# Row maxima of two key halves taken by one VectorE instruction over two PSUM banks, in the first batch of an attention and FFN kernel

## The chip, the cores and the metric

One core of a Trainium2 chip runs the whole program. The metric is the device time of one execution in microseconds (us). The engines go by their short names: PE (TensorE, matrix products), PEld (its weight loads, recorded apart), DVE (VectorE), ACT (ScalarE), POOL (GpSimd) and SP (SyncE, which issues nearly all DMAs). Matrix products land in PSUM, which this program uses as eight banks of 128 partitions by 512 fp32 numbers; the other engines read their results from there.

## The reference

Block-sparse attention over 4 batches of 8 heads (768 positions, head size 64) feeds an FFN of width 2048 with a piecewise quadratic activation.

```
scores = 0.125 * q @ k.T                 # per batch and head, 768 x 768
scores = where(mask, scores, -1e9)       # mask by blocks of 32: band, edges, 3 sampled blocks a row
scores = scores - max(scores, axis=-1)
attn = exp(scores); attn = attn / (sum(attn, axis=-1) + 1e-9)
x = (attn @ v) -> [3072, 512]
h = x @ w_in                             # 512 -> 2048
g = where(h >= 1, h, where(h <= -1, 0, (h + 1)**2 / 4))
out = g @ w_out                          # 2048 -> 512
```

## The kernel before

Precise products are made from pairs: a number is split into a rounded high part and a low remainder, and the matmuls add up high times high and the cross terms. The two weight matrices come as 64-bit numbers and are converted and split on the chip by `convert`: ACT takes an absolute value (L168), DVE does four steps on the bits (L169, L170, L172, L174) on 128x512 tiles, ACT casts to the high part (L196), DVE subtracts (L180).

**A head.** Its K and Q, with 24 rows that carry the mask, stand in tiles KA and QA, of which there are two sets, so that two heads can be in work. The load L214 brings the data, ACT casts the high part, DMAs move it into KA and QA (L221 and following), DVE forms the low part (`lo`, L228, a 128x768 subtraction). Then, for each of six query tiles of 128 rows and two halves of 384 keys, `max_mm` (L267) makes approximate scores in a PSUM bank, and `max_red` (L272) takes their maxima over the keys into one column of mc: twelve matmuls, twelve reductions. `max_col` (L276) merges the two halves into mr, `max_turn` (L280) transposes mr on PE, and `max_row` (L283) writes the negative maxima as six more rows of QA; with these rows the score matmuls subtract the maximum by themselves. In head 0 these last three steps come in two rounds of three query tiles.

Then the scores follow: for each half of 384 queries and six key tiles a pair of matmuls (L303, L304), the exponential on ACT (L308), and the value matmul (L333), which the profile records as two instructions. The six value products of a half add up in one bank, po or, for the second half in a wide head, oa2. ACT copies the result out (L351, L353); after each second head the sums are turned to reciprocals (L372, through two DMAs), and DVE and ACT make the FFN's input x from it (L387, L395).

**Heads 0 to 7, the first batch, are called wide.** No FFN runs beside them yet, since its input isn't there; the conversion of w_in runs beside them. Heads 8 to 31 run beside the FFN of the batch before, and there the maxima's banks are pa, as the scores' are.

**The FFN** (`moe`) runs in eight halves of 384 tokens: 16 tiles of the hidden width each, `l1` (L457 to L459) into hp, the activation on ACT and DVE (L463 to L478), `l2` (L485 to L487) into three output tiles oa0, oa1, oa2, one for each 128 tokens, which are kept over the 16 tiles. `o_copy` (L496, L498) copies them out by ACT; in the last half of all the second goes by DVE.

**PSUM.** Three banks pa, one po, one hp, and one each of oa0, oa1, oa2: eight. While no FFN runs, the wide heads use its banks: `bank(wide, use)` deals them out in turn, by the table RINGS (L567): scores go to oa0, oa1, hp, maxima to the three pa.

**Order.** Every step enters a list with a due time (`at`), the list is sorted by it, and a scheduler that sees dependencies and buffers sets the final order of each engine from it. An engine works its own order off without overtaking: whatever stands behind a waiting instruction waits too.

## Time and profile before

| | us |
|---|---|
| median of 3 runs | 984.24 (982.64 to 984.28) |
| the profiled execution | 983.67 |
| its span, first to last instruction | 981.8 |

Mean granted PE clock in the profiled execution: 0.998 of full speed. An instruction's row shows its start and length, its engine, its line, its output and inputs, and in brackets the idle time ahead of it on its engine with what ended that. The chain of waits goes back from the last instruction, at each step to what released it. The maxima's reductions in all heads hold 202.5 us of DVE time, of 747.5 busy. The first batch's heads lie roughly between 10 and 150 us, the first FFN half's end is at 287.6 (first output copy), and the last output copy starts at 977.65.

### The profile page before, as it was taken

Reading aid. Unit: us, or ns where it says so; the run is one execution under the profiler, and the core shown is the slowest. Engines: PE = TensorE matmul, PEld = TensorE weight load, DVE = VectorE, ACT = ScalarE, POOL = GpSimd, SP = SyncE. Lnnn points to the kernel's source line nnn. Section 1 sums busy time; section 2 is a strip of 40 time slices with the busy share of each in tenths; the row PEclk is TensorE's granted clock in tenths of the full one; section 3 lists DMA queues with packets and bytes.
Section 4 is the critical chain, followed back from the end, with each engine's and each line's share of the span. In section 5 each row is a group of like instructions: output and inputs, shape, how many; then the busy total and the mean of one; then the engine's idle time right before and its main releaser. Section 6 shows DMA issues by size and latency. Waiting matters only on the chain.

```text
span 981.8 us, 14556 instructions
## 1 busy us (share of the span) xinstructions
PE 942.5 (96%) x4687; PEld 828.1 (84%) x4687; DVE 747.5 (76%) x1403; ACT 636.5 (65%) x1302; POOL 251.8 (26%) x229
## 2 busy tenths in 40 slices
PE   5899899999889999999999999999999999999998
PEld 3666677877779899999989998998999999899997
DVE  5888999889998888978788888888888885422222
ACT  3667777677667676767677767776767676433433
POOL 1000000023334343433434343343434343000000
PEclk9999999999999999999999999999999999999999
DMA  6756677754355444645555443645445432433432
GB/s 195 205 149 189 196 209 225 259 180 139 123 182 163 145 143 133 182 139 153 159 150 182 131 150 116 199 137 175 138 142 178 125 115 89 154 130 129 160 129 97
DMA packets 56216, 154.43 MB, mean 157 GB/s; under 512 B 9612, under 2 KB 17952, under 8 KB 56140
## 3 DMA queue, kind: packets, MB, share of 16 engines
q1 hardware_dynamic: 56100, 153.48, 51.5%
q8 instruction: 37, 0.61, 0.3%
q14 instruction: 39, 0.32, 0.1%
q10 hardware_dynamic: 40, 0.03, 0.0%
HBM read 100.92 MB, written 14.81 MB: 118 GB/s over the span
## 4 chain that ended last, share of the span: by engine, by line
PE 85%; DVE 7%; ACT 3%; DMA 2%; issue 2%; SPq 0%; ACTq 0%; DVEq 0%
PE oa L485 8%; PE oa L487 8%; PE oa L486 8%; PE hp L457 8%; PE hp L459 7%; PE hp L458 7%; PE pa L267 7%; PE pa L303 5%; PE pa L304 5%; PE po L335 5%; PE po L336 4%; PE po L333 4%; DVE mc L272 2%; PE oa L333 2%; DMA QA<-qkh 1%
## 5 line engine op out<-in xcount | busy, mean ns | idle before, releaser
L323 POOL TENSOR_TENSOR acc<-acc,pt 128x384 f32<-128x384 f32 x176 | 201.7, 1146 | 233.0 <-ACT pt L308 195.1
L272 DVE TENSOR_REDUCE mc<-pa 128x1 f32<-128x384 f32 x384 | 202.5, 547 | 19.3 <-PE pa L267 16.1
L196 ACT CAST ph<-pt 128x384 fp32r<-128x384 f32 x264 | 135.5, 514 | 92.4 <-PE po L335 89.3
L316 DVE TENSOR_TENSOR pl<-pt,ph 128x384 fp32r<-128x384 f32 x264 | 163.6, 620 | 34.7 <-ACT ph L196 34.0
L308 ACT ACTIVATE pt<-pa 128x384 f32<-128x384 f32 x288 | 140.6, 489 | 54.6 <-PE pa L304 45.0
L457 PE MATMUL hp<-x,wi 128*128 128x384 f32 x448 | 155.5, 347 | 4.0 <-DVE r L469 4.0
L485 PE MATMUL oa<-w,gh 128*128 128x512 f32 x384 | 153.3, 399 | 0.3 <-ACT gh L196 0.3
L487 PE MATMUL oa<-w,gl 128*128 128x512 f32 x384 | 151.6, 395 | 0.3 <-DVE gl L478 0.3
L459 PE MATMUL hp<-x,wi 128*128 128x384 f32 x448 | 151.2, 338 | 0.0
L458 PE MATMUL hp<-x,wi 128*128 128x384 f32 x448 | 151.1, 337 | 0.0
L486 PE MATMUL oa<-w,gh 128*128 128x512 f32 x384 | 150.8, 393 | 0.0
L267 PE MATMUL pa<-KA,QA 88*128 88x384 f32 x384 | 138.3, 380 | 5.4 <-DMA QA<-qkh 3.8
L323 POOL TENSOR_TENSOR acc<-pt 128x384 f32<-128x384 f32 x44 | 46.5, 1058 | 345.5 <-ACT pt L308 345.5
L469 DVE SCALAR_TENSOR_TENSOR r<-r,hp 128x384 f32<-128x384 f32 x112 | 61.5, 549 | 73.3 <-ACT r L466 72.9
L478 DVE TENSOR_TENSOR gl<-r,gh 128x384 fp32r<-128x384 f32 x128 | 84.3, 658 | 24.0 <-ACT gh L196 23.5
L303 PE MATMUL pa<-QA,KA 102*128 102x384 f32 x288 | 99.0, 344 | 1.8 <-ACT pt L308 1.1
L463 ACT ACTIVATE r<-hp,half_c 128x384 f32<-128x384 f32 x112 | 65.1, 582 | 54.1 <-PE hp L459 51.2
L304 PE MATMUL pa<-QB,KB 128*128 128x384 f32 x288 | 97.9, 340 | 0.0
L267 PEld LDWEIGHTS pa<-KA,QA 88*128 88x128 f32 x384 | 73.1, 192 | 28.7 <-DVE mc L272 4.7
L335 PE MATMUL po<-ph,vn 128*128 128x384 f32 x264 | 91.4, 346 | 5.1 <-DVE xun L345 3.4
L457 PEld LDWEIGHTS hp<-x,wi 128*128 128x128 f32 x448 | 84.5, 189 | 10.7 <-DVE r L469 6.1
L336 PE MATMUL po<-pl,vn 128*128 128x384 f32 x264 | 88.6, 336 | 0.0
(97 smaller groups left out, 1624.3 us busy)
## 6 DMA issues: line engine op xcount, KB each, us to landing
w<-wo_dram SPq DMA_DIRECT2D x112, 512.0 KB
qk<-in_qk_t_dram SPq DMA_DIRECT2D x32, 384.0 KB
raw<-in_moe_w_in_dram SPq DMA_DIRECT2D x16, 512.0 KB
raw<-in_moe_w_out_dram SPq DMA_DIRECT2D x16, 512.0 KB
wo_dram<-w SPq DMA_DIRECT2D x16, 512.0 KB
lv<-in_v_dram SPq DMA_DIRECT2D x32, 192.0 KB
KA<-qkh SPq DMA_DIRECT2D x32, 192.0 KB
QA<-qkh SPq DMA_DIRECT2D x32, 192.0 KB
```

The source lines that it names most:

```text
L267: nc.tensor.matmul(out=pm[:, 0:HALF], lhsT=QAi[0:KM, t * 128:(t + 1) * 128], rhs=KAi[0:KM, kh * HALF:(kh + 1) * HALF], start=True, stop=True)
L272: nc.vector.reduce_max(out=st["mc"][:, t, kh:kh + 1], in_=st.pop(("pm", t, kh))[:, 0:HALF], axis=AX.X)
L303: nc.tensor.matmul(out=ps[:, 0:HALF], lhsT=KAi[0:KA, ks], rhs=QAi[0:KA, cs], start=True, stop=False)
L304: nc.tensor.matmul(out=ps[:, 0:HALF], lhsT=st["KB"][:, ks], rhs=st["QB"][:, cs], start=False, stop=True)
L316: (nc.gpsimd if i < 2 * H and c in PL1 else nc.vector).tensor_tensor(out=pl, in0=st["p", c], in1=f(st["ph", c]), op=ALU.subtract)
L323: nc.gpsimd.tensor_tensor(out=st["acc", hf], in0=prev, in1=st["p", c], op=ALU.add)
L457: nc.tensor.matmul(out=hv, lhsT=wi[:, j, 0, fs], rhs=x[:, 0], start=(j == 0), stop=False)
L458: nc.tensor.matmul(out=hv, lhsT=wi[:, j, 0, fs], rhs=x[:, 1], start=False, stop=False)
L459: nc.tensor.matmul(out=hv, lhsT=wi[:, j, 1, fs], rhs=x[:, 0], start=False, stop=(j == NP - 1))
L485: nc.tensor.matmul(out=o, lhsT=gh[:, ts], rhs=w[:, 0], start=(fi == 0), stop=False)
L486: nc.tensor.matmul(out=o, lhsT=gh[:, ts], rhs=w[:, 1], start=False, stop=False)
L487: nc.tensor.matmul(out=o, lhsT=gl[:, ts], rhs=w[:, 0], start=False, stop=(fi == NF - 1))
```

## The change

In the wide heads, `pair_mm` makes both key halves of a query tile one after the other, in two banks of a tile of three banks named oa, and `pair_red` takes the maximum over both (768 numbers a row) in one instruction, which writes the column of mr directly; `max_col` does nothing there. The due times come from the same numbers as before, one per query tile in place of one per half. The banks are shared out anew: oa0, oa1 and oa2 are one tile oa of three banks, of which there is one; in the wide heads the maxima and the transposes use it, the scores use the three pa, and the second half's values use hp. The FFN's three outputs are slices of the tile oa.

```diff
@@ bank
-            if name[0] == "o":
-                return psc.tile([128, DM], F32, name=name)
+            if name == "oa":
+                return psc.tile([128, 3, DM], F32, name="oa")
@@ head
+        def pair_mm(t):
+            if "mr" not in st:
+                st["mr"] = pr.tile([128, T], F32R, name="mr", bufs=2)
+            pm = st["pm", t] = bank(wide, "m")
+            for kh in range(2):
+                nc.tensor.matmul(out=pm[:, kh, 0:HALF], lhsT=QAi[0:KM, t * 128:(t + 1) * 128],
+                                 rhs=KAi[0:KM, kh * HALF:(kh + 1) * HALF], start=True, stop=True)
+
+        def pair_red(t):
+            nc.vector.tensor_reduce(out=st["mr"][:, t:t + 1], in_=st.pop(("pm", t))[:, 0:2, 0:HALF], axis=AX.XY, op=ALU.max)
...
         def max_col(lo=0, n=T):
+            if wide:
+                return
...
         def max_turn(lo=0, n=T):
-            pm = st["pr"] = bank(wide, "m")
+            pm = st["pr"] = bank(wide, "m")[:, 0] if wide else bank(wide, "m")
...
-        for n, (t, kh) in enumerate(jobs):
+        for t in range(T) if wide else ():
+            u = pre - (G["m0"] - G["m1"] * t / T)
+            at(u, pair_mm, t)
+            at(u + G["mr"], pair_red, t)
+        for n, (t, kh) in enumerate(jobs if not wide else ()):
...
                 if wide and hf:
-                    st["po"] = psc.tile([128, DM], F32, name="oa2")
+                    st["po"] = psh.tile([128, 512], F32, name="hp")
@@ l2
-                g["o", t] = psc.tile([128, DM], F32, name=f"oa{t}")
+                if t == 0:
+                    g["oa"] = psc.tile([128, 3, DM], F32, name="oa")
+                g["o", t] = g["oa"][:, t]
@@ tables
-RINGS = {"s": ("oa0", "oa1", "hp"), "m": ("pa", "pa")}
+RINGS = {"s": ("pa", "pa"), "m": ("oa", "oa")}
```

The program's order changes with it. First PE's order at the end of head 0, where head 1's maxima are made before its first scores. Before (L267 maxima, L333 values, L280 transpose, L303 and L304 scores):

```order
L333 MATMUL oa_348<-pl,vn 128x384
L267 MATMUL pa<-KA_116,QA_114 128x384 x2
L333 MATMUL oa_348<-pt,vn 128x384
L267 MATMUL pa<-KA_116,QA_114 128x384 x2
L333 MATMUL oa_348<-ph,vn 128x384
L267 MATMUL pa<-KA_116,QA_114 128x384 x2
L333 MATMUL oa_348<-pl,vn 128x384
L267 MATMUL pa<-KA_116,QA_114 128x384 x3
L280 MATMUL pa<-idr,mr 6x128
L303 MATMUL oa_379<-QA_114,KA_116 128x384
```

and of the change, whose lines are numbered anew (L268 maxima, L350 values, L293 transpose, L320 and L321 scores):

```order
L350 MATMUL hp<-pl,vn 128x384
L350 MATMUL hp<-pt,vn 128x384
L268 MATMUL oa<-KA_116,QA_114 128x384 x2
L350 MATMUL hp<-ph,vn 128x384
L350 MATMUL hp<-pl,vn 128x384
L268 MATMUL oa<-KA_116,QA_114 128x384 x6
L293 MATMUL oa<-idr,mr 6x128
L320 MATMUL pa<-QA_114,KA_116 128x384
```

Three whole pairs now stand behind the last value, where three single matmuls stood. DVE's order in a middle head, from the first maxima of one head to its row write; before (L272 reduction, L387, L395 the FFN's input, L372 reciprocal, L276 merge, L283 row write):

```order
L272 TENSOR_REDUCE mc<-pa 128x1 x2
L387 TENSOR_TENSOR xun<-xun,den 128x384
L272 TENSOR_REDUCE mc<-pa 128x1 x2
L395 TENSOR_TENSOR x<-xun,x 128x384
L272 TENSOR_REDUCE mc<-pa 128x1 x6
L372 RECIPROCAL rc<-rc 24x32
L272 TENSOR_REDUCE mc<-pa 128x1 x2
L170 TENSOR_SCALAR cva<-cva 128x512
L276 TENSOR_TENSOR mr<-mc 128x6
L169 TENSOR_SCALAR cva<-cva 128x512
L172 SCALAR_TENSOR_TENSOR cva<-raw,cva 128x512
L283 TENSOR_TENSOR QA_114<-pa,nd 6x768
```

and of the change from the second pair on (L404, L412 the FFN's input, L389 reciprocal, L296 row write):

```order
L272 TENSOR_REDUCE mr<-oa 128x1
L172 SCALAR_TENSOR_TENSOR cva<-raw,cva 128x512
L174 SCALAR_TENSOR_TENSOR cva<-raw,cva 128x512
L404 TENSOR_TENSOR xun<-xun,den 128x384
L272 TENSOR_REDUCE mr<-oa 128x1
...
L272 TENSOR_REDUCE mr<-oa 128x1
L228 TENSOR_TENSOR qk<-qk,qkh 128x768
L272 TENSOR_REDUCE mr<-oa 128x1
L172 SCALAR_TENSOR_TENSOR cva<-raw,cva 128x512
L296 TENSOR_TENSOR QA_114<-oa,nd 6x768
```

Conversion steps and L228 now stand between the reductions. Last, the end of PE's order, the three output slices of the last half (L504 to L506 in the change are L485 to L487 before); of the change, with the waits that stand on each row:

```order
L504 MATMUL oa<-w,gh 128x512
L505 MATMUL oa<-w,gh 128x512
L506 MATMUL oa<-w,gl 128x512
L504 MATMUL oa<-w,gh 128x512 [waits Activation_49]
L505 MATMUL oa<-w,gh 128x512
L506 MATMUL oa<-w,gl 128x512
```

The third slice's first matmul now waits for ACT, which copies the first slice out. The same wait stands at the end of each FFN half; before, there was none.

## The prediction

> **What bounds the kernel now.** I read the page first, from engine totals to the chain that ended last.

> ```profile
> PE 942.5 (96%) x4687; PEld 828.1 (84%) x4687; DVE 747.5 (76%) x1403; ACT 636.5 (65%) x1302; POOL 251.8 (26%) x229
> PE 85%; DVE 7%; ACT 3%; DMA 2%; issue 2%; SPq 0%; ACTq 0%; DVEq 0%
> L272 DVE TENSOR_REDUCE mc<-pa 128x1 f32<-128x384 f32 x384 | 202.5, 547 | 19.3 <-PE pa L267 16.1
> ```

> TensorE (PE) holds 85% of the chain, VectorE (DVE) 7%; the reductions that the change touches are 384, and those of the first batch's eight heads, 96 of them, are replaced. An average over the span says little about these heads, so the windows come next.

> ```profile
> 10.00:42.00 32.00, 26.85 (x90) 19.55 (x90) 26.38 (x53) 17.39 (x35) 0.00 (x0) 0.95 0.69 204
> 42.00:140.00 98.00, 91.32 (x376) 66.18 (x375) 86.10 (x170) 68.98 (x140) 0.00 (x0) 1.00 0.63 183
> 150.00:205.00 55.00, 54.43 (x252) 44.34 (x251) 48.65 (x96) 37.74 (x74) 0.00 (x0) 1.00 0.73 237
> 400.00:800.00 400.00, 397.41 (x2092) 366.36 (x2092) 335.67 (x628) 284.79 (x596) 159.82 (x142) 1.00 0.52 153
> ```

> The columns are window, length, busy PE, weight load, DVE, ACT, POOL, then PE clock. From 42 to 140 us PE is idle 6.7 of 98 us; from 150 on it is hardly idle at all. So VectorE time saved can buy something only before about 150 us, and there at most PE's idle time. What makes PE idle stands in the chain's pieces and the timeline:

> ```profile
> 11.45 0.67 PE pa L267
> 12.14 2.89 DVE mc L272 x6
> 16.66 0.53 PE L303 MATMUL oa<-QA,KA 102*128 102x384 f32 x1
> 29.40 5.77 DVE mc L272 x12
> 36.20 0.96 DVE QA L283
> 37.21 0.44 PE oa L303
> ...
> 53.21 0.95 DVE L283 TENSOR_TENSOR QA<-pa,nd 6x768 fp32r<-6x768 f32 x1
> 101.26 0.52 PE L280 MATMUL pa<-idr,mr 128*6 128x128 f32 x1
> 102.98 0.44 PE L303 MATMUL oa<-QA,KA 102*128 102x384 f32 x1 [1.21 <-DVE QA L283]
> 133.57 0.95 DVE L283 TENSOR_TENSOR QA<-pa,nd 6x768 fp32r<-6x768 f32 x1
> ```

> Every head ends in one chain: last maxima, their reduction, the transpose L280, the row write L283, the next head's first score L303. From transpose to score PE loses 1.72 us (101.26 to 102.98). I call the interval between two row writes a head. The first takes 17.0 (36.20 to 53.21); the five up to 133.57 take 80.4, or 16.07 each.

> PE's own work in a head:

> ```profile
> 22.99 0.81 PE L333 MATMUL po<-pl,vn 128*128 128x384 f32 x2
> 24.00 0.81 PE L333 MATMUL po<-pt,vn 128*128 128x384 f32 x2
> 24.99 0.81 PE L333 MATMUL po<-ph,vn 128*128 128x384 f32 x2
> 401.76 0.34 PE L267 MATMUL pa<-KA,QA 88*128 88x384 f32 x1
> 401.94 0.34 PE L303 MATMUL pa<-QA,KA 102*128 102x384 f32 x1
> 402.12 0.34 PE L304 MATMUL pa<-QB,KB 128*128 128x384 f32 x1
> 402.30 0.40 PE L485 MATMUL oa<-w,gh 128*128 128x512 f32 x1
> ```

> A score pair with its value takes 1.00, a maxima matmul or half a score pair 0.18. So 12 x 1.00 + 12 x 0.18 = 14.2, plus the 1.72 of the chain, is 15.9: the heads run 0.2 above the floor that PE and this chain set. That is the most that lighter reductions could give per head.

> **The price of the new reduction.** No row shows 768 elements reduced over two banks. Nearest rows of DVE, recorded mean ns:

> ```profile
> L283 DVE TENSOR_TENSOR QA<-pa,nd 6x768 fp32r<-6x768 f32 (+2 forms) x10 | 8.7, 870 | 2.6 <-PE pa L280 2.2
> L228 DVE TENSOR_TENSOR qk<-qk,qkh 128x768 f32<-128x768 f32 x8 | 7.6, 946 | 0.0
> L172 DVE SCALAR_TENSOR_TENSOR cva<-raw,cva 128x512 int32<-128x512 int32 x17 | 11.7, 687 | 0.4
> L169 DVE TENSOR_SCALAR cva<-cva 128x512 f32<-128x512 f32 x18 | 7.5, 418 | 3.3 <-ACT cva L168 3.3
> ```

> Bounds: one old reduction, 0.55, below; two, 1.09, above. I take 0.95, since both 768-element forms stand there (the L283 row at 133.57 is one of them, reading PSUM). Neighbours overlap: twelve reductions of 547 ns took 5.77, 0.48 each, so 0.07 of each record is overlap, and the new one occupies DVE for about 0.88 to 0.90. [...]

> DVE per head: before 12 x 0.48 + 0.15 (L276) = 5.9; after 6 x 0.90 = 5.4. **Half a microsecond a head** leaves DVE, 4 us over eight heads, all beside PE work unless DVE ends the head.

> **What it adds: one buffer.** The pair of maxima lies in tile oa, of which there is one. Where three pa banks let PE write on while DVE reduced, a pair's matmuls now wait for the reduction of the pair before, and the transpose for the last one. By the rows, a reduction starts when its matmul's record ends (11.45 + 0.67 = 12.12, DVE at 12.14). At full clock the second matmul of a pair ends 0.18 + 0.34 after the first starts; then 0.95 of reduction: a pair cannot follow the last sooner than **1.5 us**, where two old reductions took 0.96 and PE wrote on meanwhile. This matters where pairs stand close together in PE's order, and that is so at the start.

> *Head 0.* At half clock an issue takes 0.32 and the record 0.53 to 0.67 (row below), so a cycle is 0.32 + 0.67 + 0.95 = 1.94.

> ```profile
> 11.45 2.92 PE L267 MATMUL pa<-KA,QA 88*128 88x384 f32 x6 [2.57 <-DMA QA<-qkh]
> 33.01 1.19 PE L267 MATMUL pa<-KA,QA 88*128 88x384 f32 x3
> ```

> Three pairs from 11.45 end their reductions at 17.3 where six old ones ended at 15.03; the old merge L276 (0.16) goes, and the fourth pair slips in ahead of the scores. Transpose 17.3, row write 17.65 to 18.2, first score 18.3, against 16.7: +1.6.

> *Head 1.* In the new order its last three pairs stand in a row behind head 0's last value. In before that value is issued at about 33.3, with three single maxima still to come; shifted by 1.6, with three fewer singles ahead of it (-0.5), and with head 0's second transpose now covered by only two values (1.72 - 1.3 = +0.4), it ends at 34.8. Then 34.8, 36.3, 37.8 are the pairs, the last reduction ends at 39.4, transpose 39.45, row write 39.8 to 40.75, first score 40.8 against 37.21. **Both together +3.6.** Bounds: +1.6 if head 1 hides its tail, +5 if conversions get between.

> *The clock.* The granted clock falls after this hole already:

> ```profile
> 34.00:36.00 2.00, 0.30 (x2) 0.08 (x1) 2.00 (x6) 1.17 (x4) 0.00 (x0) 1.00 0.04 13
> 38.00:40.00 2.00, 2.00 (x9) 1.50 (x7) 2.00 (x4) 1.82 (x5) 0.00 (x0) 0.66 0.80 207
> 40.00:42.00 2.00, 2.00 (x6) 1.38 (x5) 1.91 (x4) 0.82 (x2) 0.00 (x0) 0.50 0.97 248
> ```

> It costs (1 - 0.66) x 2 + (1 - 0.50) x 2 = 1.7 us of PE work; in the head 17.0 - 16.07 = 0.9 shows. With the hole grown from 4 to 6 us (34.8 to 40.8, three short pairs in it) I take 2.1, that is 1.2 more; bounds 0 and 2.5.

> *Six middle heads.* Here two to four units of scores and values lie between pairs. I walked both new orders with these durations. Head 4 to 5, from its first score at 0: four score pairs, a value and a pair bring the first pair to 2.5; DVE comes free from conversions at 2.7, reduces to 3.95; pair 2 at 4.5, reduced 5.3 to 6.2 behind three conversion steps; pair 3 at 6.85, but behind L172, L174, L387 reduced 7.95 to 8.85; pair 4 at 9.2, reduced 10.2 to 11.1; pair 5 at 11.6, reduced 12.15 to 13.05; pair 6 at 13.2, behind L228 reduced 13.9 to 14.8; transpose 14.95, L172, row write 15.5 to 16.45: 16.5. PE is never held more than 0.1 by a pair, but the last reduction comes 0.6 after the last value. The six come to 16.15, 16.75, 15.9, 16.5, 16.05 and 16.45 = 97.8 at full clock, against 97.4 with the clock's 0.9 in it: **+1.3**. With 0.55 for a reduction the floor of 15.9 is reached, 95.4: -1.1; with 1.09 each tail grows by 0.15 to 0.4, +3.

> *Head 8 and the FFN's start.* PE is busy 54.43 of 55 us in both; three conversions come earlier, and I book **-0.3** (0 to -2).

> **The single tile under the FFN.** l2's three outputs are now slices of one tile, so a copy waits for the matmuls ahead of it in program order, and the next matmul on a slice for the copy. At a boundary between halves of the second to fourth batches:

> ```profile
> 400.76 0.59 ACT L498 COPY o<-oa 128x512 f32<-128x512 f32 x1
> 401.52 0.40 PE L487 MATMUL oa<-w,gl 128*128 128x512 f32 x1
> ...
> 976.50 0.59 ACT L498 COPY o<-oa 128x512 f32<-128x512 f32 x1 [1.29 <-PE oa L487]
> 976.54 0.39 PE L487 MATMUL oa<-w,gl 128*128 128x512 f32 x1
> 976.96 0.69 DVE L496 COPY o<-oa 128x512 f32<-128x512 f32 x1 [1.16 <-PE oa L487]
> 977.65 0.59 ACT L498 COPY o<-oa 128x512 f32<-128x512 f32 x1 [0.56 <-PE oa L487]
> ```

> The first copy moves from 400.76 to 401.95, ends 402.55, and the third slice's L485 starts 402.6 instead of 402.30: 0.3, at four boundaries where PE is full: **+1.2** (0 if other matmuls fill in, 3 if the casts queued behind the copy on ACT are late for PE too).

> *Tail.* Before, the three copies ran beside the matmuls. After: second slice done 976.95, copy 0.59, third slice's three matmuls 0.9 to 978.45, DVE copy 0.69 to 979.15, last copy 0.59 to 979.8, against 978.24: **+1.6**. No other work is left to hide it.

> **Sum:** 3.6 + 1.2 + 1.3 - 0.3 + 1.2 + 1.6 = +8.6, on the profiled execution's 983.67 (0.57 below the median of 984.24): **992.3**.

> **Rivals.**
> *A: DVE's relief shows.* If DVE ends the heads, the half microsecond comes off each, at PE's bound: 7 x -0.5 = -3.5, and at the start the shorter queue of reductions spares about 1.5 of the 5.77. With the FFN terms, -3.5 - 1.5 + 2.8 = -2.2: 981.5, faster. It decides when the pairs are reduced before the head's last value ends, so that the transpose no longer waits. For it: DVE is busy 88% of the heads and its rows stand in the chain. Against: heads are within 0.2 of PE's floor.
> *B: the buffer stalls PE in every head.* If conversions hold a reduction up by 0.4 at each of 36 pairs in six heads, PE waits 14 more: 1006. [...] The row for such waits now, us in total, times and longest:

> ```profile
> PEld pa L267 <- DVE mc L272: 3.1, 11, 0.6
> ```

> With three banks there is hardly a gap. Against B: my walk finds room between pairs.
> *C: nothing changes in the heads.* PE bounds them both ways, and the start loses little. Only the FFN terms stay: 983.67 + 2.8 = 986.5.

> **How the numbers follow.** Forecast (986.5 to 999): 0.62. A: 0.14. B: 0.10. C (984 to 987): 0.14. Low end 981, which takes A in; high end 999, the start's, clock's and FFN's upper bounds together; what lies outside is B and edges. About 0.2%, 2 us, is what a measurement of this kernel can tell from no change. Faster takes A but for its upper edge, 0.12; the same takes that edge and half of C, 0.09; slower 0.79.

> **What would show it.** Right: L272 near 0.95; head 0's first score near 18.3, head 1's near 40.8; granted clock 0.5 for some 4 us after it; three copies in a row at the end, 1.6 longer. Wrong: a reduction under 0.7 or over 1.1; head 1's first score before 38; PE idle before pairs inside the middle heads; six middle heads under 96.

## The result and the profile after

The changed kernel is slower: median 994.27 us of 6 runs (991.77 to 995.86) against 984.28 us of 6 runs of the kernel before (982.64 to 985.25). The ratio is 1.0111, 95% interval 1.0095 to 1.0127, so +10.0 us where +8.6 was forecast. A second comparison, on another chip, gave 1.0136 (1.0116 to 1.0156). The profiled execution's span grew from 981.8 to 991.4, by 9.6.

The page's totals and the chain by engine, of the changed kernel:

```profile
PE 948.5 (96%) x4687; PEld 832.6 (84%) x4687; DVE 743.2 (75%) x1346; ACT 637.3 (64%) x1302; POOL 252.5 (25%) x229
PE 87%; DVE 7%; DMA 2%; ACT 2%; issue 2%; SPq 0%; DVEq 0%; ACTq 0%
```

VectorE (DVE) did give back time: 747.5 became 743.2 us busy, 4.3 less, where "half a microsecond a head" made 4. None of it shortened the span. PE is busy 6 us longer with the same 4687 matmuls, which points to slower matmuls. The windows, same stretches as before, say where:

```profile
10.00:42.00 32.00, 22.55 (x77) 15.85 (x78) 24.55 (x37) 15.50 (x31) 0.00 (x0) 0.96 0.71 209
42.00:140.00 98.00, 91.43 (x366) 67.19 (x364) 91.37 (x145) 70.72 (x143) 0.00 (x0) 0.96 0.71 205
400.00:800.00 400.00, 398.40 (x2095) 366.38 (x2094) 335.75 (x628) 286.14 (x597) 161.60 (x143) 1.00 0.52 155
```

In the first stretch PE's busy time fell from 26.85 to 22.55 us and its instructions from 90 to 77: that is the start lagging behind. From 42 to 140 us the clock's mean is 0.96 in place of 1.00.

The new reduction, as the trace shows it (durations as least, median and most; then who waited for it, us in total and times):

```profile
L272 DVE TENSOR_REDUCE mr<-oa x48: 932/957/960, 11.6 to 139.0; 128x1 fp32r<-128x768 f32 x48
  PEld oa L268: 9.5, 14
  PEld oa L293: 6.5, 7
  PE oa L268: 4.5, 5
  PE oa L293: 3.0, 5
```

0.957 us, where 0.95 was taken. And PE now waits for it, at the next pair (L268) and at the transpose (L293).

The best single view is a ruler laid along the program: the start of each head's row write (L283 before, L296 after) in two profiles of the kernel before and in four that share the changed kernel's program up to the FFN's last halves (the changed kernel twice, and the experiments below that touch only the end). Times in us, each the difference of two starts in one profile; a star marks a stretch that a drop of PE's clock (to 0.50) made longer.

| stretch | before, two profiles | changed, four profiles | difference of means |
|---|---|---|---|
| first maxima to head 1's write | 24.75, 25.11 | 29.83, 29.36, 29.39, 31.00* | +5.0 |
| head 1 to 2 | 17.01*, 15.37 | 17.93*, 17.71*, 17.74*, 18.15* | +1.7 |
| head 2 to 7 | 80.36, 79.14 | 81.94*, 80.48, 80.51, 81.89* | +1.5 |
| head 7 to 8 | 15.70, 15.71 | 13.88, 15.51*, 15.53*, 13.90 | -1.0 |
| head 8 to 13 | 152.83, 152.67 | 155.18*, 157.24*, 154.61, 155.19* | +2.8 |
| head 13 to 31 | 505.04, 505.68 | 505.01, 503.28, 505.86, 504.45 | -0.7 |
| last write to the span's end | 174.7, 174.7 | 177.0, 177.0 (changed kernel only) | +2.3 |

The start and the end lose, the long middle, where PE is full, loses nothing, and the clock drops later show up here and there. The first maxima began at 10.1 to 11.6 us in the four and at 11.5 before, as the first data landed; on the mean that takes 0.7 off the whole time, beside the rows of the table.

### The profile page after: what moved, and what is told of

Same layout as the page of the kernel before. It is cut to its first block, busy times and chain, and to the rows that moved or that the text cites. A ratio compares the mean times of both kernels' runs of the same rounds, so it can differ in the third digit from the quotient of the medians.

```text
span 991.4 us, 14491 instructions
## 1 busy us (share of the span) xinstructions
PE 948.5 (96%) x4687; PEld 832.6 (84%) x4687; DVE 743.2 (75%) x1346; ACT 637.3 (64%) x1302; POOL 252.5 (25%) x229
## 4 chain that ended last, share of the span: by engine, by line
PE 87%; DVE 7%; DMA 2%; ACT 2%; issue 2%; SPq 0%; DVEq 0%; ACTq 0%
PE oa L504 9%; PE oa L506 8%; PE oa L505 8%; PE hp L474 8%; PE hp L475 7%; PE hp L476 7%; PE pa L320 7%; PE pa L321 7%; PE pa L278 5%; PE po L352 5%; PE po L350 5%; PE po L353 4%; PE oa L268 2%; PE hp L350 1%; PE pa L476 1%
## 5 line engine op out<-in xcount | busy, mean ns | idle before, releaser
L325 ACT ACTIVATE pt<-pa 128x384 f32<-128x384 f32 x320 | 156.1, 488 | 76.6 <-PE pa L321 63.9
L333 DVE TENSOR_TENSOR pl<-pt,ph 128x384 fp32r<-128x384 f32 x264 | 162.6, 616 | 33.7 <-ACT ph L196 32.6
L283 DVE TENSOR_REDUCE mc<-pa 128x1 f32<-128x384 f32 x288 | 155.6, 548 | 25.5 <-PE pa L278 23.7
L320 PE MATMUL pa<-QA,KA 102*128 102x384 f32 x384 | 148.2, 386 | 9.3 <-DVE QA L296 7.8
L504 PE MATMUL oa<-w,gh 128*128 128x512 f32 x384 | 154.6, 402 | 1.0 <-ACT o L517 0.7
L506 PE MATMUL oa<-w,gl 128*128 128x512 f32 x384 | 151.8, 395 | 0.3 <-DVE gl L495 0.3
L321 PE MATMUL pa<-QB,KB 128*128 128x384 f32 x384 | 133.5, 348 | 0.0
L278 PE MATMUL pa<-KA,QA 88*128 88x384 f32 x288 | 101.0, 354 | 0.9 <-ACT pt L325 0.7
L320 PEld LDWEIGHTS pa<-QA,KA 102*128 102x128 f32 x384 | 74.5, 194 | 25.0 <-DVE QA L296 10.8
L474 PEld LDWEIGHTS hp<-x,wi 128*128 128x128 f32 x448 | 85.2, 190 | 11.6 <-DVE r L486 6.6
```

Source lines behind the costliest of these rows:

```text
L283: nc.vector.reduce_max(out=st["mc"][:, t, kh:kh + 1], in_=st.pop(("pm", t, kh))[:, 0:HALF], axis=AX.X)
L320: nc.tensor.matmul(out=ps[:, 0:HALF], lhsT=KAi[0:KA, ks], rhs=QAi[0:KA, cs], start=True, stop=False)
L321: nc.tensor.matmul(out=ps[:, 0:HALF], lhsT=st["KB"][:, ks], rhs=st["QB"][:, cs], start=False, stop=True)
L325: nc.scalar.activation(out=p, in_=st.pop(("ps", c))[:, 0:HALF], func=AF.Exp, scale=SCALE)
L333: (nc.gpsimd if i < 2 * H and c in PL1 else nc.vector).tensor_tensor(out=pl, in0=st["p", c], in1=f(st["ph", c]), op=ALU.subtract)
L474: nc.tensor.matmul(out=hv, lhsT=wi[:, j, 0, fs], rhs=x[:, 0], start=(j == 0), stop=False)
```

## The experiments

### The changed kernel and the kernel before, once more

Both unchanged, for a second profile each.

> The changed kernel once more, unchanged. Its first profile had half-clock spells at 38 to 46, 106 to 112, 254 to 258 and 288 to 292 us; a kernel with the same first 300 us had them at 38 to 46 and 140 to 144 only. Theory: the first spell is set by the hole ahead of head 1's first score and is there again; the later ones fall where a wait of 1.5 to 2 us happens to lie and come at other places or not. Each costs 1.4 to 1.8 us where PE bounds. Rival (they are fixed by the program): the same four places. Time 992 to 995 in either case.

Measured: 995.1 us median (992.33 to 995.92). PE's clock in the first profile and in this one, windows of 2 us (length, busy PE with instructions, clock, DMA share, GB/s); first profile:

```profile
106.00:108.00 2.00, 0.64 (x3) 0.89 1.05 230
108.00:110.00 2.00, 2.00 (x8) 0.50 1.06 235
110.00:112.00 2.00, 2.00 (x9) 0.76 1.07 251
```

and the repeat:

```profile
106.00:108.00 2.00, 0.46 (x2) 1.00 1.10 263
108.00:110.00 2.00, 2.00 (x11) 1.00 1.03 227
110.00:112.00 2.00, 2.00 (x10) 1.00 1.06 226
```

The same program, the same hole ahead of head 5's first score (PE busy 0.64 and 0.46 of 2 us), and once the clock drops, once not. The repeat had its drops at 38 to 46, 140 to 145 and 288 to 296 us. The long one at 38 to 46 came in all four profiles; the others take turns. Head 5 to 6 lasts 17.71 with the drop and 16.31 without, head 7 to 8 15.51 and 13.88: about 1.5 us each.

> The kernel before, once more, for a second profile. Theory (its holes are too short for half-clock spells but for the one at 38 to 42 us): the same one spell and no other, the same head times to 0.2 us. Rival (spells fall on it by chance too): one or more after 100 us.

Measured: span 979.9, 1.9 below that of the first profile. This profile shows no drop at all before the end, though the hole ahead of head 1's first score is there:

```profile
36.00:38.00 2.00, 0.61 (x3) 0.47 (x4) 1.94 (x5) 1.39 (x2) 0.00 (x0) 1.00 0.36 98
38.00:40.00 2.00, 2.00 (x11) 1.54 (x10) 2.00 (x4) 1.72 (x5) 0.00 (x0) 1.00 0.63 164
```

Neither expectation met it whole: no drops by chance at later places, but the one at 38 to 42, which the prediction took as the kernel's own, comes and goes as well. Head 1 to 2 lasts 15.37 without it and 17.01 with it: 1.6 us, not the 0.9 that I read from the heads' mean. The other heads up to 8 repeat to 0.1 us but for head 3 to 4, which takes 16.66 and 15.53 at full clock in both.

### Work for PE in the hole

```diff
+        def warm(k, n):
+            if "wm" not in st:
+                st["wm"] = pso.tile([128, 512], F32, name="po")
+            pm = st["wm"]
+            for _ in range(n):
+                nc.tensor.matmul(out=pm[0:k, 0:HALF], lhsT=f(st["mr"])[:, 0:k], rhs=VW[0][:, 0:3], start=True, stop=True)
...
             at(u, pair_mm, t)
+            if i == 1 and t > 2:
+                at(u + 0.01, warm, t, 1)
...
+        if i == 1:
+            at(pre - G["mt"] + 0.01, warm, T, 2)
```

> The changed kernel with five more matmuls whose results nobody reads (two instructions of about 0.65 us together at full clock each), one behind each of head 1's last three pairs and two behind its transpose, so that PE works in the hole ahead of head 1's first score. Theory (the long half-clock spell at 38 to 46 us comes of PE idling there): the spell is gone or halved; from head 1's row write to head 2's the time falls from 17.7 to 18.1 in four runs to 16.2 or 16.5; whole time -1 to -2. Rival (the clock's dip is tied to something else at that place, DMA or the first loads): the spell stays, 17.7 or more, and the time is that of the changed kernel or a little more.

Measured: 993.28 us, ratio 1.0098 (1.0079 to 1.0117). The hole's windows in this kernel:

```profile
38.00:40.00 2.00, 1.69 (x6) 1.00 0.52 193
40.00:42.00 2.00, 1.69 (x6) 1.00 0.76 197
42.00:44.00 2.00, 1.76 (x9) 1.00 0.98 250
```

and in the changed kernel:

```profile
38.00:40.00 2.00, 0.81 (x3) 0.82 0.54 171
40.00:42.00 2.00, 0.56 (x2) 0.50 0.99 238
42.00:44.00 2.00, 2.00 (x8) 0.50 1.02 260
44.00:46.00 2.00, 2.00 (x6) 0.50 0.79 151
```

With PE kept busy the drop is gone, and head 1 to 2 falls to 16.24, where the four profiles of the table have 17.71 to 18.15; that is the walk's 16.15 at full clock. So the drop at this place follows from PE's idle time, and costs 1.7 us here. In the whole time the gain is not sure: the intervals of 1.0098 and 1.0111 overlap, and this execution had drops at 108 and 286 us of its own. It also lost the gain again in head 4 to 5, which took 18.23 where the four profiles have 16.6: at clock 1.00, PE was busy 14.6 us in it, so that 3.6 us were idle in place of 1.7. The order was planned anew with the five matmuls in it. The drops may be a part of why the changed kernel's runs spread over 4 us; that is not shown.

PE need not stand idle all the while for a drop: it was busy 1.58 and 1.68 of the 3.41 us (46 and 49%) ahead of the drops at 107.55 us in the changed kernel and at 38.66 in the kernel before. The last section shows where the 3.41 us come from.

### Two buffers for the pairs

```diff
-    psa = pool("psa", 3, space=PSUM)
-    psc = pool("psc", 1, space=PSUM)
+    psa = pool("psa", 2, space=PSUM)
+    psc = pool("psc", 2, space=PSUM)
...
-                return psc.tile([128, 3, DM], F32, name="oa")
+                return psc.tile([128, 2, DM], F32, name="oa")
...
-                if t == 0:
-                    g["oa"] = psc.tile([128, 3, DM], F32, name="oa")
-                g["o", t] = g["oa"][:, t]
+                if t != 1:
+                    g["oa"] = psc.tile([128, 2, DM], F32, name="oa")
+                g["o", t] = g["oa"][:, t % 2]
```

> The changed kernel with the pairs in two tiles of two banks that take turns, and two pa banks in place of three (the eight banks allow no more); the FFN's outputs lie in these two tiles. Theory (one buffer makes PE wait for each reduction where pairs stand in a row): in head 0 the second pair is issued while the first is reduced, pairs come every 1.0 to 1.3 us in place of 2.05, and the first score stands 2 us sooner behind the first pair (5.9 us in place of 7.86); the idle stretch ahead of head 1's first score shrinks from 7 to 4 or 5 us, that score comes near 38, and the half clock after it is shorter. What two pa banks cost in the heads beside the FFN is open, 0 to +20 in the whole time. Rival (conversions ahead of the reductions on VectorE set the start, not the buffer): first score still 7.5 us or more behind the first pair, head 1's first score still past 40.

Measured: 1011.88 us, ratio 1.0313 (1.0286 to 1.034). The total is lost mostly behind the start: the distance to the kernel before is 8.0 us at head 8, of which 5.1 come between heads 7 and 8, and grows steadily to 25.9 at head 31. There pa has two banks in place of three and the FFN's outputs lie in two tiles; this run doesn't part the two. The start is what was asked. PE's timeline there, in the changed kernel:

```profile
10.60 0.98 PE L268 MATMUL oa<-KA,QA 88*128 88x384 f32 x2 [2.25 <-DMA QA<-qkh]
12.63 1.01 PE L268 MATMUL oa<-KA,QA 88*128 88x384 f32 x2 [1.05 <-DVE mr L272]
14.69 1.01 PE L268 MATMUL oa<-KA,QA 88*128 88x384 f32 x2 [1.05 <-DVE mr L272]
18.46 0.52 PE L320 MATMUL pa<-QA,KA 102*128 102x384 f32 x1
...
34.39 0.62 PE L268 MATMUL oa<-KA,QA 88*128 88x384 f32 x2 [0.15 <-DVE mr L272]
36.06 0.62 PE L268 MATMUL oa<-KA,QA 88*128 88x384 f32 x2 [1.05 <-DVE mr L272]
37.92 0.62 PE L268 MATMUL oa<-KA,QA 88*128 88x384 f32 x2 [1.23 <-DVE mr L272]
39.59 0.27 PE L293 MATMUL oa<-idr,mr 128*6 128x128 f32 x1 [1.05 <-DVE mr L272]
41.44 0.69 PE L320 MATMUL pa<-QA,KA 102*128 102x384 f32 x1 [1.58 <-DVE QA L296]
```

and with two buffers:

```profile
10.52 1.62 PE L268 MATMUL oa<-KA,QA 88*128 88x384 f32 x4 [2.14 <-DMA QA<-qkh]
12.55 1.01 PE L268 MATMUL oa<-KA,QA 88*128 88x384 f32 x2 [0.41 <-DVE mr L272]
16.32 0.52 PE L320 MATMUL pa<-QA,KA 102*128 102x384 f32 x1
...
33.01 0.81 PE L268 MATMUL oa<-KA,QA 88*128 88x384 f32 x2
35.34 0.22 PE L293 MATMUL oa<-idr,mr 128*6 128x128 f32 x1 [1.52 <-DVE mr L272]
36.92 0.69 PE L320 MATMUL pa<-QA,KA 102*128 102x384 f32 x1 [1.36 <-DVE QA L296]
```

With one buffer, pairs come every 2.05 us at half rate, 1.7 to 1.9 at full, behind an idle 1.05 to 1.23 that the reduction ends. (In head 0 the half rate is read from the matmuls, one every 0.32 us in place of 0.18, as from 41.92 on, where the clock column reads 0.50; in head 0 it reads 1.00.) With two, the first two pairs run through; head 0's first score stands 5.8 us behind the first maxima instead of 7.86, and head 1's at 36.92 instead of 41.44. Head 1's row write stands 25.4 behind the first maxima, against 24.75 and 25.11 before the change. So 4.5 of the start's 5.0 us come back with the second buffer. In head 0 that is the buffer; in head 1 it is not one cause alone, since with two buffers the planner also spreads the last pairs among the values. Heads 1 to 7 gained nothing: 100.5 us, against 98.2 to 100.0 in the four profiles.

### The end

Two ways to part copies and matmuls. First only the copies, placed behind all three slices:

```diff
-            at(t0 + (NF + G["l2"] - 1) * p + (t + 1) * p * G["l3"] + 0.05, o_copy, t)
+            at(t0 + (NF + G["l2"] - 1) * p + 3 * p * G["l3"] + 0.05 + 0.01 * t, o_copy, t)
```

> The changed kernel, but the three output copies of each FFN half are placed behind the matmuls of all three slices, so that no slice's matmul waits for a copy. Theory (the single tile ties copies and matmuls): the nine last matmuls run through in 2.36 us as before the change, then two ACT copies of 0.59 in a row: 3.6 us from the first of them to the end of the last copy plus nothing else, against 4.84 (983.09 to 987.93) in the changed kernel, so about -1.2: 993.1. Theory on the seven inner boundaries: the trace shows no loss there from 302 to 814 us, so no further gain. Rival (each boundary costs 0.2 to 0.3 that is hidden in the other differences): 991.5 or less.

Measured: 992.49 us, ratio 1.0105 (1.0085 to 1.0124), not to be told from the changed kernel. The matmuls do run through, but the three copies then follow one another, ACT, DVE, ACT; from the first of the nine matmuls (981.91) to the last copy's end (986.33) it takes 4.4 us, not 3.6. Copies of one tile's slices by two engines don't overlap in this program: they start at 984.40, 985.02 and 985.75 and take 0.58, 0.69 and 0.58.

Second, three separate banks in the last half:

```diff
+                if end and t == 0:
+                    g["o", t] = psc.tile([128, 3, DM], F32, name="oa")[:, 0]
+                elif end:
+                    g["o", t] = (pso, psa)[t - 1].tile([128, 512], F32, name=("po", "pa")[t - 1])
+                else:
```

> The changed kernel, but in the very last half the three outputs of the FFN lie in three separate banks (one of oa, po, one of pa), free there since no attention runs. Theory (at the end the single tile puts copies and the third slice's matmuls in one row): first of the nine last matmuls to end of the last copy falls from 4.84 back to 3.0, as before the change, -1.9 us; against the repeat of the changed kernel on the same chip 0.998 of its time. Rival (the last copy is late for another reason, ACT busy with the activation): 4 us or more stay.

Measured: 992.63 us, ratio 1.0113 (1.0096 to 1.013), beside 995.1 and 1.0136 of the changed kernel on the same chip; the two intervals overlap, so the trace has to carry the reading. The copies of the changed kernel and the matmul that waits among them:

```profile
984.91 0.58 ACT L517 COPY o<-oa 128x512 f32<-128x512 f32 x1 [1.87 <-PE oa L506]
...
985.55 0.50 PE L504 MATMUL oa<-w,gh 128*128 128x512 f32 x1 [0.68 <-ACT o L517]
...
986.61 0.69 DVE L515 COPY o<-oa 128x512 f32<-128x512 f32 x1 [2.98 <-PE oa L506]
987.34 0.59 ACT L517 COPY o<-oa 128x512 f32<-128x512 f32 x1 [1.84 <-DVE o L515]
```

and with separate banks:

```profile
985.50 0.59 ACT L522 COPY o<-oa 128x512 f32<-128x512 f32 x1 [1.29 <-PE oa L511]
985.96 0.69 DVE L520 COPY o<-po 128x512 f32<-128x512 f32 x1 [1.16 <-PE po L511]
986.65 0.58 ACT L522 COPY o<-pa 128x512 f32<-128x512 f32 x1 [0.56 <-PE pa L511]
```

The nine matmuls begin at 983.09 and 984.26, so the end takes 4.84 and 2.97 us: 1.87 is the single tile's price, as expected to a few hundredths. From the last row write to the span's end it is now 175.3, against 177.0 in the changed kernel and 174.7 before. The 0.6 that are left fit the two boundaries between FFN halves in this stretch, where no attention fills in any more: in this run the weight loads of the third slice wait 0.3 for a copy at each of the two.

### VectorE's share: two instructions per pair

```diff
-            nc.vector.tensor_reduce(out=st["mr"][:, t:t + 1], in_=st.pop(("pm", t))[:, 0:2, 0:HALF], axis=AX.XY, op=ALU.max)
+            pm = st.pop(("pm", t))
+            for kh in range(2):
+                nc.vector.reduce_max(out=st["mc"][:, t, kh:kh + 1], in_=pm[:, kh, 0:HALF], axis=AX.X)
```

The merge L276 is back as well.

> The changed kernel's banks, pairs and single buffer, but each pair is reduced by two instructions of 384 and merged as before the change. Theory (buffer): what is lost stays, since a pair is held as long: two times 0.48 + 0.07 is 1.03 in place of 0.96, and L276 adds 0.15 to each head's chain; 0 to +3 on the changed kernel, 994 to 997. Rival 1 (the long reduction itself delays, a first short one could start behind the first matmul): 0.2 to 0.3 per pair comes back at the start, 3 us in all, 991. Rival 2 (VectorE's saved time does count in the middle heads): half a microsecond per head is lost, +4, 998.

Measured: 1008.41 us, ratio 1.0262 (1.0232 to 1.0292): some 14 us on the changed kernel, more than any of the three expected. The planner had put the last pair behind the last value in heads 1, 2, 3 and 6 (in the changed kernel only in head 1), and VectorE's order shows what stands there:

```profile
59.06 0.68 DVE L180 TENSOR_TENSOR wi<-cva,wi 128x512 fp32r<-128x512 f32 x1
59.66 0.69 DVE L172 SCALAR_TENSOR_TENSOR cva<-raw,cva 128x512 int32<-128x512 int32 x1
60.27 1.02 DVE L274 TENSOR_REDUCE mc<-oa 128x1 f32<-128x384 f32 x2
61.20 0.33 DVE L389 RECIPROCAL rc<-rc 24x32 f32<-24x32 f32 x1
61.45 0.09 DVE L289 TENSOR_TENSOR mr<-mc 128x6 fp32r<-128x6 f32 x1
```

Two conversion steps ahead of the last reductions, a reciprocal ahead of the merge: PE waits 1.79 us for the transpose at 61.61 and 1.34 more for the score at 63.17, the clock drops behind it (from 63.66 on the score matmuls start 0.32 us apart in place of 0.18), and four of the heads have such a drop (17.9 to 20.2 us each). So the one long reduction isn't worthless in this layout. But the reductions and the planned order changed together here, and the 14 us can't be parted into them.

### VectorE's share: fewer conversion steps

```diff
-            nc.vector.tensor_scalar(out=a, in0=a, scalar1=3, scalar2=0x3FFFFFFF,
-                                    op0=ALU.logical_shift_left, op1=ALU.bitwise_and)
-            nc.vector.scalar_tensor_tensor(out=a, in0=hi32, scalar=-0x40000000, in1=a,
-                                           op0=ALU.bitwise_and, op1=ALU.bitwise_or)
```

In the kernel before and in the changed one.

> The kernel before, leaving out the same two conversion steps. Theory (PE and the chain set the heads, VectorE does not): the six heads from 36 to 134 us fall from 16.2 to 15.9 at most, and the whole time by 2 to 4 us, a part of it from the stretch from 210 to 300 us, where VectorE is busy 95%: 978 to 982. Rival A of the prediction (VectorE ends the heads): each falls by 1 us or more, 974 or less.

Measured: 979.12 us, ratio 0.9973 (0.9956 to 0.9989). From 42 to 140 us VectorE is now busy 78.7 of 98 us in place of 86.1, and the heads are no shorter: head 1 to 7 takes 100.9, with two drops of the clock in it (at 38 and 106 us), against 97.4 and 94.5; head 1 to 2 takes 18.8 of it, the others 15.7 to 16.6 each. The gain comes from behind: head 11 to 12 falls from 37.8 to 30.5, where w_out is converted beside the FFN. Rival A's ground is gone as far as one run shows it: with less work on VectorE the first batch's heads are no shorter. The order was planned anew here too.

> The changed kernel, leaving out two of VectorE's five steps in every weight conversion (L170 and L172, about 1 us each time), so the weights are not the reference's. It takes 2 to 3 us per head off VectorE in the first batch. Theory (buffer and chain: pair, reduction, next pair, transpose): the start hardly moves, head 1's first score stays 3 us or more behind that of the light kernel before, and the whole difference to it stays 6 us or more. Rival (conversions that stand between the reductions on VectorE make the loss): head 1's first score within 1.5 us, whole difference under 4.

Measured: 987.21 us, ratio 1.0055 (1.0035 to 1.0074). Against the light kernel before, 8.1 us are left, and head 1's first score is at 40.68 against 36.69, 4.0 later; counted from the first maxima to head 1's row write it is 28.45 against 24.06, 4.4 more. The loss survives with a fifth of VectorE's work in these heads taken out (91.4 to 74.1 us), most of it at least.

### Pairs earlier

```diff
-            u = pre - (G["m0"] - G["m1"] * t / T)
+            u = pre - (G["m0"] - G["m1"] * t / T) - (PAIR_UP if i else 0.0)
...
+PAIR_UP = 1.0
```

> The changed kernel with the pairs and their reductions due one step (about 1.3 us) earlier in heads 1 to 7. Theory (in the middle heads the last reduction comes about 0.6 us after the last value, so that the transpose waits): the transpose comes with the last value, heads go from 16.3 without the clock's part to 15.9, -2 to -3 over six heads: about 991.5. Rival (VectorE is full with conversions there, 91.4 of 98 us, and sets the heads): no change, 994.

Measured: 1001.13 us, ratio 1.0197 (1.0176 to 1.0218): by the ratios some 8 us worse than the changed kernel, and neither expectation holds. The longest of the heads is 5 to 6, 21.75 us where the four profiles have 16.3 to 17.8. The line that tells why, from PE's timeline, at head 6's first pair:

```profile
117.97 0.59 PE L268 MATMUL oa<-KA,QA 88*128 88x384 f32 x2 [1.82 <-DMA QA<-qkh]
```

The first pair now stands in PE's order ahead of the landing of its own QA rows, and everything behind it waits, 1.82 us here; the clock drops after that (the score matmuls at 121.47 and 121.79 start 0.32 us apart in place of 0.18). There the pairs can't move up unless their data do. Heads 2 to 3 and 3 to 4 are longer too (18.47 and 18.36, the second with a drop at 79 us, against 15.6 and 15.9), where PE waits for a DMA no more than 0.4 us; their loss is not traced to a cause.

## Why the prediction was right

Time and sign were right: 992.3 forecast, 994.27 measured, inside 981 to 999, and the mechanism, one buffer where there were three, is shown for the start by the experiment with two. That 8.6 came so near 10.0 is in part luck: the start was 1.4 short and the clock 2 to 3, while the FFN boundaries' 1.2 hardly showed, the middle of the program came out 0.7 shorter, and the first data landed 0.7 sooner on the mean. By its own steps:

- **The price of the reduction, 0.95, and half a microsecond a head off DVE:** 0.957 and 4.3 us in all. That it lies beside PE's work: the heads didn't shorten even when VectorE lost two conversion steps.
- **Start, +3.6:** head 1's first score came at 41.44 for 40.8 forecast, but from first maxima that began at 10.60 in place of 11.45; counted from these the loss is 5.0. Cycle 1.94 forecast, 2.05 measured; at full clock 1.5 forecast, 1.7 to 1.9 measured, since a pair's rows end 0.62 after it starts and not 0.52, each hand-over takes some 0.05, and a conversion (L180) holds one reduction up by 0.2.
- **The clock, +1.2:** the mechanism was right and its size wrong. The drop behind head 1's hole came in all four profiles, where before it came in one of two profiles, and costs 1.7 there. The step overlooked that the shorter holes of the later heads and the one near 286 us drop the clock too, now one and now another: 1.5 us in head 5 to 6 or head 7 to 8 in each of the four profiles, and 1.8, 3.1, 0 and 1.8 behind 286 us (heads 12 to 13 against 29.44 without a drop). That is 1.7 + 1.5 + 1.7, less the 0.8 that one drop in two profiles makes before: some 4 us as an upper end. Two of the profiles also dropped near 255 us and lost nothing by it (head 11 to 12 36.84 with the drop, 37.7 and 38.0 without), so that heads 8 to 13 are on the mean only 0.9 longer than in the profile without any drop there; with 0.9 for the last 1.7 it is some 3 us. Either way it is the largest miss of the sum.
- **Six middle heads, +1.3:** at full clock 16.24 (from the warmed kernel), 15.62, 15.86, 16.62, 16.31 and 16.07 make 96.7, where the walk gave 97.8; before, 94.5 and, less the drop's 1.6, 95.7 (the two differ by head 3 to 4). That is +1.0 to +2.2. The walk was 1.1 long, mostly in head 2 to 3 (16.75 for 15.62). The floor of 15.9 a head that it leant on was none: heads 1 to 2, 2 to 3 and 3 to 4 of the kernel before took 15.37, 15.28 and 15.53 in its second profile.
- **Head 8 and the FFN's start, -0.3:** head 7 to 8 got 1.8 shorter without a drop, and heads 8 to 13 gave 1.9 back (154.61 against 152.7). No net change.
- **FFN boundaries, +1.2:** nothing to be seen while attention runs. Head 13 to 31 takes 504.7 on the mean against 505.4, with single profiles up to 2.6 apart. At a boundary near 410 us the planner had put two approximate scores and a score pair between the second and the third slice, so the copy was all but hidden behind them; the lower bound, "0 if other matmuls fill in", was the case. In the last batch, with no attention left, the forecast 0.3 a boundary shows, twice.
- **Tail, +1.6:** 4.84 less 2.98, 1.86.

Rival A fell with the light kernels and C with the start. Rival B fell with one row of the changed kernel's waits from 40 to 140 us (total, times, longest):

```profile
PEld oa L268 <- DVE mr L272: 2.5, 8, 0.4
```

That is 2.5 us for all middle heads together, where B wanted 14. The transposes waited longer than the pairs, as the walk had it (0.6 a head); from the same view:

```profile
PEld oa L293 <- DVE mr L272: 3.5, 5, 1.1
```

What stays open: how much of the middle heads' +1 to +2 is the buffer and how much the new order of conversions, since no kernel changed one without the other.

## What to carry to other kernels

The wider instruction needed a wider tile here and was paid for in buffers: 4.3 us of VectorE's time gained, 5.0 lost at the start. So count how many tiles are left in the ring before counting the saved instructions, and look at the places where producers stand in a row (the first head, the end of a head) rather than at the steady part. Don't join outputs into one tile unless they are written and read together: at the end of this program nothing hid the wait, 1.87 us. And when holes on PE grow, price the clock behind them too (a drop cost 1.5 to 1.7 us in the heads here), not only at the one place where the profile happens to show a drop.

## What had not been expected of the hardware

Whether PE's clock drops at a given hole differs from one execution to the next: one program, with PE busy 0.64 and 0.46 of the same 2 us, dropped to 0.50 once and stayed at 1.00 once, for 1.4 us of difference; and the kernel before kept 1.00 with 0.61 busy where another execution of it had dropped at the same place. One profile can therefore be off by 1 to 3 us at a few places, which is as much as most terms of such a sum. From the windows' means, half speed was held for 3.4 us at 106 us (0.22 + 1.0 + 0.48 us lost, twice that held) and for 6.7 at 38 to 46.

```profile
104.14:107.55 3.41, 1.58 (x7) 1.00 1.03 321
107.55:110.96 3.41, 3.41 (x11) 0.50 1.04 233
```

and the repeat, with the steps counted from its own drop at 39.30:

```profile
104.15:107.57 3.42, 1.78 (x7) 1.00 1.05 340
107.57:110.98 3.41, 3.21 (x15) 1.00 1.03 223
```

In the first the hole ends with the score at 107.50, inside one step; in the second the score comes at 107.77 and the hole reaches into the next. In the kernel before, the hole near 36 us left PE busy for 1.68 us of one step, and the drop followed; in its second profile the hole lay across two steps with 1.95 and 2.10 us busy, and none came. In all twelve profiles from 22 us on, outside the drops, a drop followed 30 of the 31 steps in which PE was busy for less than half, 6 of the 57 between 0.5 and 0.65, and none of the 3255 above that. The ends of matmuls are modelled, so these shares are rough. In these profiles a hole's price thus depended on how it lay on this grid, and two executions of one program lay on it differently (above: a drop after a step with 1.58 us busy, none after one with 1.78).
